# Three of a batch's short float32 runs on the tensor engine are joined to others in a one-core attention and two-MLP kernel

## The chip, the cores and the metric

One core of one Trainium2 chip runs the program. The metric is the device time of one execution in microseconds (us).

## What is computed

Eight batches of attention feed two MLPs in float32. In attention 32 packed queries `p` of each head attend to `k` and `v`; the packed result then serves as keys and values of the attention of `q`:

```python
p_packed = sm_attn(p, k, v)          # 8 batches, 8 heads, 32 rows, 64 wide
out = sm_attn(q, p_packed, p_packed) # 576 rows a head
x = out.transpose(0, 2, 1, 3).reshape(B * S, H * D)   # 4608 x 512
h = x @ w_in                                          # 512 x 2048
g = where(h >= 1, h, where(h <= -1, 0, (h + 1) ** 2 / 4))
x = g @ w_out                                         # 2048 x 512
h = x @ w2_in
y = (h / (1 + exp(-h))) @ w2_out
```

## The kernel before

The MLPs' float32 products are made of three matmul passes over float32r pieces (a high and a low part of each operand). Attention's own matmuls are plain float32.

**Stage A** holds attention and the first MLP. `w_in` is multiplied by `pp` (the packed result) once a batch, so `x @ w_in` needs only the second attention's weights `a2` as its other operand. The stage runs as 256 steps, 32 a batch (16 blocks of 128 columns of `w_in`, for each half `t` of the batch's 576 rows). A step holds one block `h` (`a_h`, 6 matmuls into one PSUM bank) and one block `y` (`a_y`, 12 matmuls that add into four banks of a second pool). Between them work ScalarE (`a_relu`: relu and square; `a_hi`) and VectorE (`a_max`, which is the last to read the bank of `h`; `a_lo`). Block `y` of a step uses what block `h` of four steps earlier made. At the last `y` of a half `t`, `a_y` also copies its four banks out: two copies on VectorE, two on ScalarE.

**Attention of the next batch** is threaded through these steps as a list of slots, one slot a step. `front` has the packed queries: `s1_8` and `s1_end8` (scores), `s1_copy`, `s1_max`, `s1_exp`, transposes `s1_tr` and `s1_trt`, `et_copy` and `ett_copy`, `pp_mm`, `pp_norm`, `pp_tr`, `pp_out`. `back8` has the second attention: scores `s2_8` and `s2_end8`, then transposes and a softmax on VectorE and ScalarE (`t_in` to `t_a2`). `wps` has four pairs of `wp8` (`pp` with 512 columns of `w_in`) and `wp_out` (its split into high and low). All of them, and block `h`, take their PSUM banks with `bank()` from one pool of four (`ps_h`): `s1_8`, `s2_8` and `wp8` take two banks each, `s1_end8`, `s2_end8`, each `s1_tr`, `s1_trt`, `pp_mm` and `pp_tr` one.

**Order.** Each engine takes its instructions in one queue, in an order written out by hand: every piece of work gets a key (its step and a fraction), and all are sorted by key. Within step `n`, `h` and what follows it have fractions from 0.30, attention's slots 0.6 and block `y` with its copies 0.9. So a slot's matmuls stand between an `h` and a `y`. For a batch `b` that begins at step `base + 32`, `G['pf']` is the step, counted from `base`'s batch, of the first slot of `front`, `G['pb']` that of `back8` and `G['pw']` that of the first `wp8`. The same numbers set the steps of the loads (`load_p`, `load_k` four steps ahead of `front`, `load_v` one, `load_win` three ahead of `wp8`). During stage A the weights of the second MLP are also converted and split by ScalarE and VectorE, at steps of their own (`conv_a`, `conv_b`, `a_first` to `a_fourth`).

**Stage B**, the second MLP, follows and is not touched.

Of the kernel before, what the change touches and what calls it, by code (L numbers as in the profile page):

```python
# [72 lines left out]
def attention_then_two_mlps(ctx: ExitStack, tc: tile.TileContext, kT, vv, qT, pT, w_in, w_out, w2_in, w2_out, out):  # L73
# [3 lines left out]
    B, P, NJ, S = kT.shape  # L77
# [13 lines left out]
    NF = DFF // FW  # L91
# [27 lines left out]
    pb = const.tile([P, NJ, N2], F32, name="pbd")  # L119
# [128 lines left out]
    def att_jobs(b):  # L248
# [337 lines left out]
        def J(fn, *a):  # L586
            return lambda: fn(*a)
# [8 lines left out]
            ]),  # L596
            [J(s1_copy, 1), J(s1_max, 0)],
            [J(s1_exp, 0), J(s1_max, 1)],
            [J(s1_exp, 1), J(s1_tr, 0)],
            [J(et_copy, 0), J(s1_tr, 1), J(s1_trt)],  # L600
            [J(et_copy, 1), J(ett_copy), J(s1_rec)],
            [J(pp_mm, 0), J(pp_mm, 1)],
            [J(pp_norm)],
            [J(pp_tr)],
# [1 line left out]
        ]  # L606

        back8 = [
            [J(s2_8)],
            [J(t_in, 0), J(t_in, 1), J(s2_end8)],  # L610
            [J(t_max, 0), J(t_in, 2)],
            [J(t_exp, 0), J(t_max, 1)],
            [J(t_norm, 0), J(t_exp, 1)],
# [157 lines left out]
    def unit_h(i, p, j):  # L771
        return 2 * U * i + 14 * (p // 2) + 2 * j + p % 2

    def unit_o(i, j, p):
        return 2 * U * i + U + NPR * j + p
# [160 lines left out]
                eng.dma_start(out[r:r + P, t, TO[i]:TO[i + 1]], sb.pop(((i, 0, d), name)))  # L936


    G = dict(pf1=4, pb1=18, w1=0, pf=2, pb=16, pw=21, lw=3, lk=4, lv=-1, lq=6, ai=34, ad=25, oraw=1)
    starts = {b: (0,) if b else (0, KF // 2) for b in range(B)}  # L940
    steps = []
    for b in range(B):
# [3 lines left out]
    SPB = 2 * KF  # L946
# [5 lines left out]
    def at(n, fn, *args):  # L952
        ev(n + 0.6, fn, *args)
# [4 lines left out]
    def slots(n, jobs, every=1):  # L958
        for i, slot in enumerate(jobs):
            for fn in slot:  # L960
                at(n + i * every, fn)

    with tc.manual_schedule():
# [3 lines left out]
        for _ in range(10):  # L967
            nc.tensor.matmul(warm[:, :P], ident, ident, start=True, stop=True)
        front, back, wps = att_jobs(0)

        def fill(n, own):
# [36 lines left out]
        def W(f, k, g):  # L1008
            return (f"W{f}.{k}.{g}", wps[f][k][g])
# [63 lines left out]
        for g in range(NG):  # L1073
            for k in range(2):
                n, fn = W(1, k, g)
                job(n, 2 + 0.1 * k + 0.01 * g, fn)
        for f in range(2, NF):
            for g in range(NG):
                for k in range(2):
                    n, fn = W(f, k, g)  # L1080
                    job(n, 4 * f + k + 0.6, fn)
        for i, key in enumerate(ins[2 * KD:]):
            n = i + 3
# [3 lines left out]
        for m in range(4, KF):  # L1087
            n = m - 3 if m < KF // 2 else m + G['oraw'] + 1
            key = ("o", m)
# [10 lines left out]
        def plan_front(b, n):  # L1100
            at(n - G['lk'], load_p, b)
            at(n - G['lk'], load_k, b)
            for g in range(NG):
                at(n + G['lv'] + g, load_v, b, g)
            slots(n, jobs[b][0])

        def plan_back(b, n):
            for g in range(NG + 1):
                at(n - G['lq'] + min(g, 1), load_q8, b, g)
            slots(n, jobs[b][1]())  # L1110

        jobs = {b: att_jobs(b) for b in range(1, B)}
        plan_front(1, G['pf1'])
        plan_back(1, G['pb1'])
# [4 lines left out]
        for b in range(2, B):  # L1119
            base = (b - 1) * SPB  # L1120
            plan_front(b, base + G['pf'])
            plan_back(b, base + G['pb'])
            for f in range(NF):
                n = base + G['pw'] + 4 * f
                for g in range(NG):
                    at(n - G['lw'], load_win, b, f, g)
                slots(n, jobs[b][2][f])
# [34 lines left out]
        for i in range(NBK):  # L1162
            for k in range(2):
                for t in range(2):
                    n = NA - 31.4 + 2 * k + t if i == 0 else K0 + 2 * U * (i - 1) + 4 + 4 * (2 * k + t) + 0.95
# [11 lines left out]
            for p in range(NPR):  # L1177
                b = unit_h(i, p, 0)
# [4 lines left out]
                if p % 2:  # L1183
                    for x, name in enumerate(("t1", "t2", "t3", "t4")):
                        n = unit_o(i, 0, 2) + x if p == NPR - 1 else b + 14 + x // 2
                        bu(n, 20 + x % 2, t_sum, i, p // 2, name)
                for j in range(7):
                    n = unit_o(i, j, p)
# [77 lines left out]
```

## Time and profile before

| what | us |
|---|---|
| time before, median of 3 runs | 1445.77 (1445.53 to 1446.64) |
| the profiled execution's own time | 1445.66 |
| its span | 1443.6 |
| TensorE (PE) busy | 1429.9 |
| VectorE (DVE) busy | 951.3 |
| ScalarE (ACT) busy | 766.2 |

Rows that begin with a time give the start in us from the span's start, how long the merged instructions took, the engine, the line of the kernel, the operation, output and inputs by the program's names, shapes and the count. In brackets stands idle time just ahead of it on that engine, and what ended it. Matmuls are pipelined, so the distance of two starts says what a block cost; the length printed is longer by the last one's tail.

### The profile page before, as it was taken

To read this page: it belongs to the slowest core of one execution; us is meant where nothing else is said; L and a number is where in the kernel's file an instruction comes from. 1 tells how busy PE (TensorE), PEld (TensorE's weight loads), DVE (VectorE), ACT (ScalarE), POOL (GpSimd) and SP (SyncE) were. 2 spreads that over 40 slices of the span, in tenths; PEclk is the share of its full clock that TensorE was granted. 3 is DMA by queue.
4 is the path that set the end of the run, shared out by engine and by line. 5 is a ranking of instruction groups with operands and counts; after the bars stand their busy time and mean duration, and the time that the engine had idled before them with its cause. 6 is when DMAs were issued, how large, how long until landed. Compare 5 with 4: busy or idle time off the path is not lost.

```text
span 1443.6 us, 26352 instructions
## 1 busy us (share of the span) xinstructions
PE 1429.9 (99%) x9812; PEld 1280.5 (89%) x9812; DVE 951.3 (66%) x1711; ACT 766.2 (53%) x1536; POOL 74.8 (5%) x116
## 2 busy tenths in 40 slices
PE   8999999999999999999999999999999999999999
PEld 7778989989899898999998888888888889999998
DVE  5788586675867758577736775477646764774664
ACT  4776667676676767766653452334423541362342
POOL 0250000000000000000000000000000000000000
PEclk9999999999999999999999999999999999999999
DMA  9654545646464555545337677866787678888886
GB/s 346 230 199 131 195 163 185 230 156 222 153 223 162 187 179 190 192 156 185 105 93 241 193 208 222 267 191 193 230 258 195 193 222 281 260 269 285 253 252 223
DMA packets 178639, 300.32 MB, mean 208 GB/s; under 512 B 28624, under 2 KB 76752, under 8 KB 178512
## 3 DMA queue, kind: packets, MB, share of 16 engines
q1 hardware_dynamic: 167760, 264.36, 58.2%
q0 software_dynamic: 9344, 33.04, 6.7%
q8 instruction: 78, 1.28, 0.4%
q10 hardware_dynamic: 1408, 1.25, 0.3%
q14 instruction: 49, 0.40, 0.1%
HBM read 244.97 MB, written 53.61 MB: 207 GB/s over the span
## 4 chain that ended last, share of the span: by engine, by line
PE 90%; DVE 5%; DMA 2%; issue 1%; ACT 1%; POOL 0%; DVEq 0%; ACTq 0%; POOLq 0%
PE ps_y L707 25%; PE ps_o L904 24%; PE ps_h L842 22%; PE ps_h L661 12%; PE ps_wp L573 2%; PE ps_y L703 1%; PE ps_pp L364 1%; DMA qt<-qT 1%; DMA raw<-w_in 1%; DVE g L692 1%; DMA va<-vv 1%; PE ps_s L270 0%; DVE u L682 0%; DVE gt L887 0%; DVE w L154 0%
## 5 line engine op out<-in xcount | busy, mean ns | idle before, releaser
L707 PE MATMUL ps_y<-g,w_o 128*128 128x288 f32 x2976 | 443.8, 298 | 3.0 <-DVE g L692 1.8
L707 PEld LDWEIGHTS ps_y<-g,w_o 128*128 128x128 f32 x2976 | 407.7, 188 | 35.1 <-ACT u L676 10.1
L842 PE MATMUL ps_h<-y,a2r 128*128 128x512 f32 (+1 forms) x1680 | 347.7, 367 | 0.4 <-DVE p L868 0.2
L904 PE MATMUL ps_o<-g,a2r 128*128 128x512 f32 (+1 forms) x1680 | 345.8, 367 | 0.0
L842 PEld LDWEIGHTS ps_h<-y,a2r 128*128 128x128 f32 x1680 | 305.2, 188 | 40.9 <-DVE p L868 1.8
L904 PEld LDWEIGHTS ps_o<-g,a2r 128*128 128x128 f32 x1680 | 305.7, 188 | 39.2
L661 PE MATMUL ps_h<-a,wp 128*128 128x288 f32 x1536 | 246.2, 296 | 1.1 <-DVE u L682 0.4
L682 DVE SCALAR_TENSOR_TENSOR u<-ps_h,u 128x288 f32<-128x288 f32 x256 | 116.1, 455 | 160.2 <-ACT u L677 159.8
L661 PEld LDWEIGHTS ps_h<-a,wp 128*128 128x128 f32 x1536 | 217.3, 188 | 4.4 <-issue 1.6
L676 ACT ACTIVATE u<-ps_h,half 128x288 f32<-128x288 f32 x256 | 128.2, 501 | 171.4 <-PE ps_h L661 147.5
L677 ACT ACTIVATE u<-u 128x288 f32<-128x288 f32 x256 | 113.8, 445 | 8.1
L692 DVE TENSOR_TENSOR g<-u,g 128x288 fp32r<-128x288 f32 x240 | 109.6, 457 | 1.7 <-ACT g L686 1.7
L686 ACT CAST g<-u 128x288 fp32r<-128x288 f32 x248 | 103.5, 417 | 0.2 <-PE ps_y L703 0.2
L800 DVE TENSOR_TENSOR g<-gs,g 128x1024 fp32r<-128x1024 f32 (+1 forms) x80 | 86.7, 1112 | 7.4 <-ACT g L799 7.4
L863 ACT COPY p<-ps_h 128x512 f32<-128x512 f32 (+1 forms) x40 | 21.8, 545 | 124.1 <-PE ps_h L842 116.2
L799 ACT CAST g<-gs 128x1024 fp32r<-128x1024 f32 (+1 forms) x80 | 73.9, 962 | 8.6 <-PE ps_o L904 5.8
L868 DVE TENSOR_TENSOR p<-ps_h,p 128x512 f32<-128x512 f32 (+1 forms) x80 | 50.2, 633 | 39.9 <-PE ps_h L842 39.4
L800 DVE TENSOR_TENSOR g<-gt,g 128x1024 fp32r<-128x1024 f32 (+1 forms) x60 | 64.5, 1112 | 6.8 <-ACT g L799 6.8
L878 ACT ACTIVATE gs<-u 128x512 f32<-128x512 f32 (+1 forms) x40 | 23.6, 589 | 82.6 <-DVE u L868 82.6
L878 ACT ACTIVATE gs<-ps_h 128x512 f32<-128x512 f32 (+1 forms) x40 | 22.3, 556 | 63.3 <-PE ps_h L842 63.3
L799 ACT CAST g<-gt 128x1024 fp32r<-128x1024 f32 (+1 forms) x60 | 53.8, 963 | 0.5 <-PE ps_o L904 0.5
L645 POOL DMA_DIRECT2D win<-win_dram x48 | 25.5, 532 | 515.1 <-DVE g L692 113.2
(142 smaller groups left out, 1145.0 us busy)
## 6 DMA issues: line engine op xcount, KB each, us to landing
a2r<-a_dram SPq DMA_DIRECT2D x280, 256.0 KB, 3.0
a2r<-o_dram SPq DMA_DIRECT2D x280, 256.0 KB, 3.0
win<-win_dram POOLq DMA_DIRECT2D x48, 512.0 KB, 4.3
raw<-w_in SPq DMA_DIRECT2D x32, 512.0 KB, 7.4
raw<-w_out SPq DMA_DIRECT2D x32, 512.0 KB, 6.3
a_dram<-a2w SPq DMA_DIRECT2D x56, 256.0 KB, 2.8
o_dram<-a2w SPq DMA_DIRECT2D x56, 256.0 KB, 2.7
y_dram<-ysb SPq DMA_DIRECT2D x36, 288.0 KB, 2.5
```

Of the source, the lines that this page charges most:

```text
L661: nc.tensor.matmul(ps[:, :HB], w[:, i, o:o + P], a2[:, k, g, :], start=(n == 0), stop=(n == 3 * NG - 1))
L676: nc.scalar.activation(u, h_ps[s][:, :HB], AF.Relu, bias=half, scale=0.5)
L677: nc.scalar.activation(u, u, AF.Square)
L682: nc.vector.scalar_tensor_tensor(u, h_ps.pop(s)[:, :HB], 1.0, u, op0=ALU.max, op1=ALU.min)
L686: nc.scalar.copy(g[:, 0], u_t[s])
L692: eng.tensor_tensor(g[:, 1], u_t.pop(s), g[:, 0].bitcast(F32), op=ALU.subtract)
L707: nc.tensor.matmul(acc["y"][d][:, :HB], w[:, i, d * P:(d + 1) * P], g[:, k], start=(first and n == 0), stop=(last and n == 2),)
L799: nc.scalar.copy(hi, src)
L800: nc.vector.tensor_tensor(lo, src, hi.bitcast(F32), op=ALU.subtract)
L842: nc.tensor.matmul(ps, w[:, x, a * P:(a + 1) * P], b_t[i, j][k][:, a], start=(n == 0 and j in FIRST), stop=(n == 3 * KH - 1), skip_group_c ...
L868: nc.vector.tensor_tensor(t, bk[*key, b][:, :w], x, op=ALU.add)
L904: nc.tensor.matmul(ps, w[:, x, d * P:(d + 1) * P], g[k][:, p % 2], start=(p == 0 and n == 0 and j in FIRST), stop=(p == NPR - 1 and n == 2 ...
```

## The change

For batches 1 to 7 both groups of transposes and `s1_trt` are in one slot, and all three copies of their results in the next. `s2_end8` is in the slot of `s2_8`. For batches 2 to 7 `front` begins three steps earlier (`pf` from 2 to -1), its loads with it. For batches 2 to 6 the last `wp8`, with its load and its `wp_out`, goes from step 33 to step 38 of the batch, the slot of the next batch's `pp_mm`.

```diff
             [J(s1_exp, 0), J(s1_max, 1)],
-            [J(s1_exp, 1), J(s1_tr, 0)],
-            [J(et_copy, 0), J(s1_tr, 1), J(s1_trt)],
-            [J(et_copy, 1), J(ett_copy), J(s1_rec)],
+            *([
+                [J(s1_exp, 1), J(s1_tr, 0)],
+                [J(et_copy, 0), J(s1_tr, 1), J(s1_trt)],
+                [J(et_copy, 1), J(ett_copy), J(s1_rec)],
+            ] if b < 1 else [
+                [J(s1_exp, 1)],
+                [J(s1_tr, 0), J(s1_tr, 1), J(s1_trt)],
+                [J(et_copy, 0), J(et_copy, 1), J(ett_copy), J(s1_rec)],
+            ]),
             [J(pp_mm, 0), J(pp_mm, 1)],
...
         back8 = [
-            [J(s2_8)],
-            [J(t_in, 0), J(t_in, 1), J(s2_end8)],
+            [J(s2_8), J(s2_end8)],
+            [J(t_in, 0), J(t_in, 1)],
             [J(t_max, 0), J(t_in, 2)],
...
-    G = dict(pf1=4, pb1=18, w1=0, pf=2, pb=16, pw=21, lw=3, lk=4, lv=-1, lq=6, ai=34, ad=25, oraw=1)
+    G = dict(pf1=4, pb1=18, w1=0, pf=-1, pb=16, pw=21, lw=3, lk=4, lv=-1, lq=6, ai=34, ad=25, oraw=1)
...
             for f in range(NF):
-                n = base + G['pw'] + 4 * f
+                n = base + (G['pw'] + 4 * f if f + 1 < NF or b + 1 == B else SPB + G['pf'] + 7)
                 for g in range(NG):
                     at(n - G['lw'], load_win, b, f, g)
                 slots(n, jobs[b][2][f])
```

How the instructions stand on TensorE where batch 2 (the first is batch 0) ends its second half (the last `y` of a half reads `w_o_15`). Before, that `y` follows straight on its `h`, and no attention stands there:

```order
L661 MATMUL ps_h_4169<-a2_3841,wp_0_0_3850 128x288 [waits DVE_49]
L661 MATMUL ps_h_4169<-a2_3841,wp_0_0_3850 128x288 x2
L661 MATMUL ps_h_4169<-a2_3841,wp_1_0_3853 128x288 x3
L707 MATMUL ps_y_3617<-g_4088,w_o_15_1291 128x288 [waits Activation_49]
L707 MATMUL ps_y_3617<-g_4088,w_o_15_1291 128x288 x2
L707 MATMUL ps_y_3618<-g_4088,w_o_15_1291 128x288 x3
L707 MATMUL ps_y_3619<-g_4088,w_o_15_1291 128x288 x3
```

In the changed kernel (lines from 602 on have numbers higher by 6) the first scores of batch 4 stand between the two, in `ps_s1_4190`, `ps_s1_4191` and `ps_s1e_4200`; the next `h` is `ps_h_4234`:

```order
L667 MATMUL ps_h_4169<-a2_3841,wp_1_0_3853 128x288 x3
L270 MATMUL ps_s1_4190<-kt_4034,pbd_89 32x512 [waits DMAHW3_49,DMAHW1_49,DVE_49]
L270 MATMUL ps_s1_4191<-kt_4034,pbd_89 32x512 [waits DMAHW2_49,DVE_49]
...
L281 MATMUL ps_s1e_4200<-kte_4036,pbd_89 32x64 [waits DMAHW4_49,DVE_49]
L281 MATMUL ps_s1e_4200<-kte_4036,pbd_89 32x64 x7
L713 MATMUL ps_y_3626<-g_4096,w_o_15_1291 128x288 [waits Activation_49]
L713 MATMUL ps_y_3626<-g_4096,w_o_15_1291 128x288 x2
L713 MATMUL ps_y_3627<-g_4096,w_o_15_1291 128x288 x3
L713 MATMUL ps_y_3628<-g_4096,w_o_15_1291 128x288 x3
L713 MATMUL ps_y_3629<-g_4096,w_o_15_1291 128x288 x3
L667 MATMUL ps_h_4234<-a2_3841,wp_0_1_3993 128x288 [waits DVE_49]
```

The scores moved from behind the third `h` after that `y` to ahead of it; between `ps_h_4169` and `ps_h_4234` three banks of the pool of four are now taken.

On ScalarE at the same place, in the changed kernel, two copies of that last `y` (L722) stand ahead of the relu (L682) of `ps_h_4169`, and the first copies of the scores (L304, L308) behind it:

```order
L722 COPY ysb_4217<-ps_y_3627 128x288
L722 COPY ysb_4227<-ps_y_3629 128x288
L682 ACTIVATE u_4241<-ps_h_4169,half_86 128x288
L683 ACTIVATE u_4241<-u_4241 128x288
L692 CAST g_4244<-u_4176 128x288
L304 COPY s_4187<-ps_s1_4190 128x512
L308 COPY s_4187<-ps_s1e_4200 128x2x64
```

Before, the two copies and this relu stand in the same order; only the score copies are new here.

On VectorE of the changed kernel, at the same place, two copies (L725) stand ahead of the maximum (L688) of `ps_h_4169`, the last reader of its bank:

```order
L725 COPY ysb_4217<-ps_y_3626 128x288
L725 COPY ysb_4227<-ps_y_3628 128x288
L698 TENSOR_TENSOR g_4179<-u_4135,g_4179 128x288
L688 SCALAR_TENSOR_TENSOR u_4241<-ps_h_4169,u_4241 128x288
L698 TENSOR_TENSOR g_4244<-u_4176,g_4244 128x288
```

That order, too, is the one of before; what moved is on TensorE.

## Rows read from the trace of the kernel before

**Rows 1.** The page: busy time by engine, granted clock by slice, the chain by engine.

```profile
PE 1429.9 (99%) x9812; PEld 1280.5 (89%) x9812; DVE 951.3 (66%) x1711; ACT 766.2 (53%) x1536; POOL 74.8 (5%) x116
...
PEclk9999999999999999999999999999999999999999
...
PE 90%; DVE 5%; DMA 2%; issue 1%; ACT 1%; POOL 0%; DVEq 0%; ACTq 0%; POOLq 0%
```

**Rows 2.** Timeline of PE, first attention of batch 4: scores (L270, L281), transposes (L329, L335).

```profile
325.18 0.96 PE L661 MATMUL ps_h<-a,wp 128*128 128x288 f32 x6
326.07 1.09 PE L270 MATMUL ps_s<-kt,pbd 64*32 64x512 f32 x16
327.09 0.43 PE L281 MATMUL ps_s1e<-kte,pbd 128*32 128x64 f32 x16
327.45 1.85 PE L707 MATMUL ps_y<-g,w_o 128*128 128x288 f32 x12
329.14 0.96 PE L661 MATMUL ps_h<-a,wp 128*128 128x288 f32 x6
...
331.54 0.96 PE L661 MATMUL ps_h<-a,wp 128*128 128x288 f32 x6
...
336.32 0.96 PE L661 MATMUL ps_h<-a,wp 128*128 128x288 f32 x6
...
339.18 0.96 PE L661 MATMUL ps_h<-a,wp 128*128 128x288 f32 x6
339.97 0.60 PE L329 MATMUL ps_et<-ident,s 128*128 128x128 f32 x4
340.41 0.38 PE L335 MATMUL ps_ett<-ident,s 128*64 128x128 f32 x2
...
342.21 0.96 PE L661 MATMUL ps_h<-a,wp 128*128 128x288 f32 x6
```

**Rows 3.** Timeline of PE, second scores of batch 4: `s2_8` (L484), `s2_end8` (L495).

```profile
363.46 0.96 PE L661 MATMUL ps_h<-a,wp 128*128 128x288 f32 x6
364.35 1.09 PE L484 MATMUL ps_s<-qt,pp 64*32 64x512 f32 x16
...
367.06 0.96 PE L661 MATMUL ps_h<-a,wp 128*128 128x288 f32 x6
367.95 0.43 PE L495 MATMUL ps_s2e<-qte,pp 128*32 128x64 f32 x16
...
370.00 0.96 PE L661 MATMUL ps_h<-a,wp 128*128 128x288 f32 x6
```

**Rows 4.** Timeline of all engines, last `y` of batch 2's second half and its copies.

```profile
317.60 1.75 PE L707 MATMUL ps_y<-g,w_o 128*128 128x288 f32 x12
...
318.58 0.40 ACT L716 COPY ysb<-ps_y 128x288 f32<-128x288 f32 x1 [1.37 <-PE ps_y L707]
...
319.38 0.40 ACT L716 COPY ysb<-ps_y 128x288 f32<-128x288 f32 x1 [0.40 <-PE ps_y L707]
...
319.68 0.51 ACT L676 ACTIVATE u<-ps_h,half 128x288 f32<-128x288 f32 x1
...
320.69 0.46 DVE L682 SCALAR_TENSOR_TENSOR u<-ps_h,u 128x288 f32<-128x288 f32 x1 [0.89 <-ACT u L677]
```

**Rows 5.** Groups by line: the copies on ScalarE (busy, mean ns, idle before, releaser).

```profile
L716 ACT COPY ysb<-ps_y 128x288 f32<-128x288 f32 x32 | 12.8, 400 | 36.4 <-PE ps_y L707 36.2 <-PE ps_y L703 0.3
```

**Rows 6.** Timeline of DVE beside the second scores of batch 4.

```profile
364.97 0.46 DVE L682 SCALAR_TENSOR_TENSOR u<-ps_h,u 128x288 f32<-128x288 f32 x1 [0.89 <-ACT u L677]
```

**Rows 7.** Timeline of all engines, second scores of batch 1.

```profile
107.67 1.06 PE L661 MATMUL ps_h<-a,wp 128*128 128x288 f32 x6
...
109.20 0.44 DVE L682 SCALAR_TENSOR_TENSOR u<-ps_h,u 128x288 f32<-128x288 f32 x1
...
109.70 0.43 PE L495 MATMUL ps_s2e<-qte,pp 128*32 128x64 f32 x16 [0.97 <-DVE u L682]
```

**Rows 8.** Waits of PE's weight loads, 90 to 720 us: total, times, longest.

```profile
PEld ps_wp L573 <- DVE u L682: 2.2, 4, 1.1
```

## The prediction

> **What bounds the kernel now.** I read the page first: TensorE is busy 1429.9 us of the span and the chain that ended last is 90% PE [rows 1]. What counts is therefore whatever TensorE's queue does between two blocks; work on the other engines costs time only where TensorE waits for it. The granted clock is 9 tenths or more in all 40 slices [rows 1], the higher of its two levels (2.4 GHz), so no term below is a matter of clock.
>
> Then I read TensorE's timeline as distances of starts. An `h` and a `y` with nothing between take 331.54 - 329.14 = 2.40 us [rows 2]. Whatever a pair with an attention run inside takes beyond 2.40 is the price of that run, its way in and out included.
>
> Last I looked for the waits behind TensorE: which reader frees the PSUM bank that the next `h` wants, and what is queued ahead of this reader on VectorE and ScalarE.
>
> **The change part by part.** No matmul is added or removed. Three joints a batch go, and each has a price of its own.
>
> *Second scores in one run.* Split, they cost 367.06 - 363.46 - 2.40 = 1.20 and 370.00 - 367.06 - 2.40 = 0.54 us [rows 3], 1.74 together. The first scores have the same shapes and are already joined: 329.14 - 325.18 - 2.40 = 1.56 [rows 2]. Joining saves 0.18. But `s2_end8` now needs a third bank at once, that of the `h` before last. VectorE's maximum frees it at 364.97 + 0.46 = 365.43 [rows 6], and with the lag of 0.06 from such a release to PE (109.20 + 0.44 to 109.70 [rows 7]) the matmuls start at 365.49. Unhindered they would start 1.02 after `s2_8` (327.09 - 326.07 [rows 2]), at 365.37. That gives back 0.12. Net 0.06 in each of batches 2 to 7: 0.4 us saved, bounds 0 and 6 x 0.18 = 1.1.
>
> *Transposes in one run.* The run of four cost 339.18 - 336.32 - 2.40 = 0.46, that of six 342.21 - 339.18 - 2.40 = 0.63 [rows 2]. Inside a run one transpose takes (340.41 - 339.97) / 4 = 0.11, so ten are worth 1.10 and the two runs cost 1.09. There is no price of a joint here: 0 saved, at most 0.18 a batch if the price of the tiled runs held.
>
> *Last `wp8` beside `pp_mm`.* Both are runs on parts of the array, as the scores are, so I take the same 0.18, five times (batches 2 to 6): 0.9 saved, bounds 0 and 0.9. `wp_out` now comes one step after this run, and the first `h` that reads it a good half step later; between stand `pp_mm`, two `y` and an `h`, at least 2.40 + 1.61 = 4.0 us (below for the 1.61), which hide its two copies and two subtractions. I cost this wait at nothing; splits later than that would cost what they are late, five times. Its load keeps its lead of three steps.
>
> The Trainium skill, "TensorEngine Tiling (Array Packing)", Key Properties, says that changing the tiling mode drains the engine, not the mere step to another tile. By that, `s2_8` to `s2_end8` and `wp8` to `pp_mm` are still changes of mode (64x32 to 128x32 tiles), and a joint would save one border of two, 0.09; the sum would come out 1.0 us higher. The row disagrees in size: the joined first scores hold that same border and are cheaper by the whole 0.18.
>
> *Batch 1.* Its second scores fall where VectorE is behind. Before, an `h` ran at 107.67 and `s2_end8` waited until 109.70 for the maximum that ends at 109.64 [rows 7]. Now the two change places, and this `h` waits for it. It starts 2.03 later, less the 0.54 that `s2_end8` took and the 0.97 of wait that goes [rows 7]: up to 0.5 us worse. Below, -0.2 (only the joint saved). I take +0.4.
>
> *`front` three steps earlier.* This is the part that I find dear. Its first slot moves from step 2 to step -1, that is, to between the last `h` and the last `y` of a half. The first scores take three of four banks and that last `h` holds the fourth. The next `h` must therefore wait until VectorE has taken the maximum of the `h` just ahead of the scores; the order rows show it waiting for VectorE. Where the scores stood before, the maximum had time. Here it is queued behind the copies of the last `y`: ScalarE's relu stands behind two copies, which wait for that `y` (32 such copies idle 36.2 us for PE [rows 5]), and VectorE's maximum waits for relu and square.
>
> The times: `y` starts at 317.60, the second copy on ScalarE at 319.38, the relu at 319.68, the maximum ends at 320.69 + 0.46 = 321.15 [rows 4], 3.55 after the start of `y`. Before, nobody waited for it. Now `y` leaves a tiled run, which makes it 329.14 - 327.45 = 1.69 long instead of 1.61 (a pair's 2.40 less an `h` of 339.97 - 339.18 = 0.79) [rows 2], so the copies come 0.08 later as well and the maximum ends 3.63 after the start of `y`; with the lag of 0.06, `h` starts at 3.69. TensorE is there at 1.69. **Wait: 2.00 us.** Nothing else can run meanwhile, for `h` heads an in-order queue; behind it are the first `y` of the new half and all the rest. ScalarE and VectorE stand idle too, so nothing is caught up.
>
> This holds for the starts of `front` of batches 3 to 7, five places: 10.0 us, between 5 x 1.86 (no lag, no slower `y`) = 9.3 and 5 x 2.2 = 11 (if the first matmul after a gap adds a tenth or two). Batch 2 is spared: there batch 0 ends, whose second half is added up on VectorE (`part_t`), ScalarE copies nothing, and the order gives the next `h` a bank that `s1_copy` frees.
>
> *Loads.* Keys, values and `p` move on SP's queue by the same three steps, past the stores of `ysb` and of the second MLP's weights; their leads stay, four steps (9.6 us) for keys. I cost them at nothing; a late key load would add its lateness once a batch.
>
> **Sum**, against the profiled execution's own 1445.66: +10.0 - 0.4 - 0 - 0.9 + 0.4 = +9.1, 1454.8 us; the median shown lies 0.11 higher, so I say **1454.9**. With the bounds: 9.3 - 1.1 - 1.3 - 0.9 - 0.2 = +5.8, and 11 + 0.5 = +11.5.
>
> **Rivals.**
>
> *The joints are worth what the change counts on, and nothing waits.* Each of 7 + 7 + 5 = 19 joints saves 0.18, 3.4 us: 1442.3, faster by 0.24%. For it: the 0.18 is real for tiled runs. Against: the transposes' rows, and it needs a maximum that ends 2 us sooner than the rows say; it decides if the next `h` in fact gets another bank, or if ScalarE takes the relu ahead of the copies.
>
> *No wait, joints at my prices*: -0.4 - 0.9 + 0.4 = -0.9, 1444.8, no change that can be told.
>
> *The wait and a backlog.* `s1_max`, `wp_out` and `pp_norm` now meet other steps of the weights' conversion on VectorE. Where its queue already runs over, TensorE waits up to 1.1 us at one place [rows 8]. Two such places more: 1457.1.
>
> **How the numbers follow.** What a measurement here can tell from no change is about 0.2%, 2.9 us. My forecast gets 0.74, the backlog 0.10, both slower; the full joints without a wait 0.08, faster; no wait at my prices 0.08, same. So faster 0.08, same 0.08, slower 0.84. The range runs from 1451.5 (the lower bound, +5.8) to 1457.3 (the upper bound and the backlog at two places); the two cases without a wait lie below it.
>
> **What the profile after would show.** Right: five gaps on PE of about 2.0 us ahead of `h`, released by VectorE's maximum (L688), each about 1.7 after the start of a half's last `y`, and hardly elsewhere; the joined second scores 1.6 to 1.7 beyond a plain pair; ten transposes at 1.1; no gap ahead of the `h` that first reads the moved `wp_out`. Wrong: `h` follows that `y` without a gap (then the bank or ScalarE's order is not as I read it), the transposes' joint saves a tenth or more, or the granted clock falls behind the new gaps, which would lengthen everything after them.

## The result, and the profile after

The changed kernel takes **1460.59 us** (median, 1460.1 to 1462.51) against 1446.09 before in the same comparison: a ratio of 1.0103, 95% interval [1.0085, 1.012]. That is 14.5 us slower where 9.1 were forecast, and above the range. The profiled execution is the longest of these, 1462.51 us, 16.85 above that of before.

The page after; its rows answer to [rows 1]:

```profile
PE 1432.1 (98%) x9812; PEld 1282.1 (88%) x9812; DVE 951.3 (65%) x1711; ACT 766.2 (52%) x1536; POOL 75.1 (5%) x116
...
PEclk9999999999999999999999999999999999999999
...
PE 87%; DVE 6%; DMA 3%; ACT 2%; issue 2%; POOL 0%; DVEq 0%; ACTq 0%; POOLq 0%
```

PE is only 2.2 us busier (1429.9 before) in a span that is 17.1 longer: all of the loss but these 2 us is waiting. Who is waited for stands in the view of PE's waits, 90 to 740 us (total, times, longest):

```profile
PE ps_h L667 <- DVE u L688: 11.3, 7, 1.9
...
PE ps_s2e L495 <- DVE u L688: 1.4, 1, 1.4
PE ps_s1e L281 <- DVE u L688: 1.3, 1, 1.3
```

Before, the same view has one short wait of `h` for the maximum (L682 there):

```profile
PE ps_h L661 <- DVE u L682: 0.4, 1, 0.4
```

Five of the seven waits are the predicted places, 1.86 us each; the sixth, 1.59, is at batch 1's second scores, and the last is the short one of before. No `h` waits for the moved `wp_out`, as predicted. Line numbers behind the changed lists are six higher than before: the maximum is L688, the relu L682, the copies of `ysb` L722 and L725. One of the five predicted places in the timeline of all engines, the start of batch 4's `front` (it answers to [rows 2] and [rows 4]):

```profile
323.16 1.09 PE L270 MATMUL ps_s<-kt,pbd 64*32 64x512 f32 x16
...
324.18 0.43 PE L281 MATMUL ps_s1e<-kte,pbd 128*32 128x64 f32 x16
324.54 1.85 PE L713 MATMUL ps_y<-g,w_o 128*128 128x288 f32 x12
...
325.62 0.40 ACT L722 COPY ysb<-ps_y 128x288 f32<-128x288 f32 x1 [2.92 <-PE ps_y L713]
...
326.42 0.40 ACT L722 COPY ysb<-ps_y 128x288 f32<-128x288 f32 x1 [0.40 <-PE ps_y L713]
326.72 0.51 ACT L682 ACTIVATE u<-ps_h,half 128x288 f32<-128x288 f32 x1
...
327.73 0.46 DVE L688 SCALAR_TENSOR_TENSOR u<-ps_h,u 128x288 f32<-128x288 f32 x1 [0.89 <-ACT u L683]
...
328.24 1.06 PE L667 MATMUL ps_h<-a,wp 128*128 128x288 f32 x6 [1.86 <-DVE u L688]
329.14 1.08 PE L713 MATMUL ps_y<-g,w_o 128*128 128x288 f32 x7
```

`y` starts at 324.54; relu follows ScalarE's second copy; the maximum ends at 328.19, 3.65 after the start of `y` (predicted: 3.63); `h` starts 3.70 after it (predicted: 3.69). Where nothing hinders it that is 1.69, so the wait is 2.01. The other four starts of `front` (at 234.84, 417.23, 506.94 and 601.14) show 3.70, 3.71, 3.70 and 3.75. The `h` itself then takes 329.14 - 328.24 = 0.90 in place of 0.80.

The joined runs on PE's timeline: ten transposes, `wp8` with `pp_mm` (both batch 4), second scores (batch 4; they answer to [rows 3]):

```profile
337.91 0.96 PE L667 MATMUL ps_h<-a,wp 128*128 128x288 f32 x6
338.71 1.03 PE L329 MATMUL ps_et<-ident,s 128*128 128x128 f32 x8
339.58 0.38 PE L335 MATMUL ps_ett<-ident,s 128*64 128x128 f32 x2
...
341.39 0.96 PE L667 MATMUL ps_h<-a,wp 128*128 128x288 f32 x6
...
343.79 0.96 PE L667 MATMUL ps_h<-a,wp 128*128 128x288 f32 x6
344.68 1.09 PE L573 MATMUL ps_wp<-win,pp 64*32 64x512 f32 x16
...
349.05 0.96 PE L667 MATMUL ps_h<-a,wp 128*128 128x288 f32 x6
...
370.81 0.96 PE L667 MATMUL ps_h<-a,wp 128*128 128x288 f32 x6
371.70 1.09 PE L484 MATMUL ps_s<-qt,pp 64*32 64x512 f32 x16
372.83 0.43 PE L495 MATMUL ps_s2e<-qte,pp 128*32 128x64 f32 x16
...
374.88 0.29 PE L667 MATMUL ps_h<-a,wp 128*128 128x288 f32 x1
```

Beyond a plain pair of `h` and `y` (2.40): transposes 341.39 - 337.91 - 2.40 = 1.08 (split: 1.09); second scores 374.88 - 370.81 - 2.40 = 1.67 (split: 1.74), where `s2_end8` starts 1.13 behind `s2_8` in place of 1.02; `wp8` with `pp_mm` 349.05 - 343.79 - 2.40 = 2.86, where the trace of before has 1.20 and 1.87 for the two.

So the wait and the joints of batches 2 to 7 are as forecast, and more has gone elsewhere. Starts of `h` after against before, step by step, show where: +1.6 at batch 1's transposes and +0.7 at its second scores; +0.5 some steps behind the second scores of batch 2, where a `y` waits for VectorE; +1.3 at the first scores of batch 5; +1.8 at the second scores of batch 6; +1.5 behind the wait at the start of batch 6's `front`; and +1.1 ahead of step 0, where TensorE, ScalarE and VectorE still run the same instructions as before. The places at batches 5 and 6 are called late places below.

### The profile page after: what moved, and what is told of

It reads as the page before. It is cut to its first block, busy times and chain, and to the rows that moved or that the text cites. A ratio compares the mean times of both kernels' runs of the same rounds, so it can differ in the third digit from the quotient of the medians.

```text
span 1460.7 us, 26346 instructions
## 1 busy us (share of the span) xinstructions
PE 1432.1 (98%) x9812; PEld 1282.1 (88%) x9812; DVE 951.3 (65%) x1711; ACT 766.2 (52%) x1536; POOL 75.1 (5%) x116
## 4 chain that ended last, share of the span: by engine, by line
PE 87%; DVE 6%; DMA 3%; ACT 2%; issue 2%; POOL 0%; DVEq 0%; ACTq 0%; POOLq 0%
PE ps_y L713 24%; PE ps_o L910 24%; PE ps_h L848 22%; PE ps_h L667 12%; PE ps_wp L573 2%; PE ps_y L709 1%; DVE u L688 1%; DMA qt<-qT 1%; PE ps_pp L364 1%; DMA raw<-w_in 1%; DVE g L698 1%; DMA raw<-w_out 1%; ACT u L682 1%; DMA va<-vv 1%; ACT u L683 0%
## 5 line engine op out<-in xcount | busy, mean ns | idle before, releaser
L688 DVE SCALAR_TENSOR_TENSOR u<-ps_h,u 128x288 f32<-128x288 f32 x256 | 116.2, 455 | 170.9 <-ACT u L683 170.3
L682 ACT ACTIVATE u<-ps_h,half 128x288 f32<-128x288 f32 x256 | 128.2, 501 | 175.3 <-PE ps_h L667 149.1
```

Of the source, the lines that this page charges most:

```text
L682: nc.scalar.activation(u, h_ps[s][:, :HB], AF.Relu, bias=half, scale=0.5)
L688: nc.vector.scalar_tensor_tensor(u, h_ps.pop(s)[:, :HB], 1.0, u, op0=ALU.max, op1=ALU.min)
```

## The experiments

The kernel before was measured beside each. Its median was 1445.40 beside joints_only, front_only, batch1_split and relu_first; 1445.47 beside one_step_sooner, raw_early, before_relu_first and best_of_parts; and 1445.53 beside half_the_wait, before_raw_early and best_raw_early. A ratio goes by all executions and not by the two medians.

**joints_only.** `front` and the last `wp8` go back.

```diff
-    G = dict(pf1=4, pb1=18, w1=0, pf=-1, ...)
+    G = dict(pf1=4, pb1=18, w1=0, pf=2, ...)
...
-                n = base + (G['pw'] + 4 * f if f + 1 < NF or b + 1 == B else SPB + G['pf'] + 7)
+                n = base + (G['pw'] + 4 * f if f + 1 < NF or b + 1 == B else G['pw'] + 4 * f)
```

> The two joints alone (transposes in one run, second scores in one run, batches 1 to 7); front and the last wp8 at their old places. By the prediction's terms: second scores -0.4, transposes 0, batch 1's second scores +0.4, together 0: 1446 us. By the trace of after: as that, but batch 1 pays more, its ten transposes take 2.6 us in place of 1.0 because two banks are not free yet, and its second scores net +0.7: 1447 to 1448.5. Rival, each joint worth the 0.18 us of a tiled run: 14 x 0.18 less, 1443.6.

Measured: 1448.04 us (1447.51 to 1449.69), ratio 1.0019 [1.001, 1.0028]. None of the five waits is there, and no joint is worth 0.18. In batches 2 to 7 the starts of `h` move by 0.00 at the transposes (+0.47 from one run, -0.47 from the other) and by -0.07 at the second scores. What is lost is 2.3 us in batch 1 and 0.5 behind batch 2's second scores. This 0.5 is in the trace of every kernel that joins batch 2's scores, and not in front_only. As the traces read, the next `h` comes later behind the joined scores, VectorE stands idle 0.5 us longer there and then has work without a gap until a `y` waits for it; no run tests this reading.

**front_only.** The reverse: `front` and `wp8` moved, the slots of transposes and second scores as before, for all batches.

```diff
-            ] if b < 1 else [
+            ] if b < B else [
                 [J(s1_exp, 1)],
...
-            [J(s2_8), J(s2_end8)],
-            [J(t_in, 0), J(t_in, 1)],
+            [J(s2_8)],
+            [J(t_in, 0), J(t_in, 1), J(s2_end8)],
```

> The earlier front and the moved last wp8 alone; transposes and second scores split as before. By the prediction's terms: five waits +10.0 and -0.9: 1455.2. By the trace of after: five waits with a slower first h, 5 x 2.13 = 10.6, three late places in batches 5 and 6 of 1.3 to 1.8 each, 4.7 together, less 1.0 for wp8: +14.3, 1460.4. If the late places belong to the joined second scores and not to the moved front, one of them (1.8) goes and it is 1458.6.

Measured: 1459.6 us (1458.55 to 1462.7), ratio 1.0103 [1.0088, 1.0119], between the two figures expected. The late place at batch 6's second scores is there too, 1.0 us with split scores in place of 1.8; PE waits 0.6 ahead of batch 5's first scores. So late places come with the moved `front` or the moved `wp8`, and the joined scores make one of them dearer. The ratio is that of the whole change, but the joints still cost something: this trace has two stretches at the lower clock (told of at raw_early), and the trace of after has one behind a wait. Without such stretches, and the one ahead of step 0, the last `h` starts 11.7 us later than before here, 2.5 later in joints_only and 14.8 later in after.

**batch1_split.** After, with `b < 1` turned to `b < 2` in the list of transposes, and the same choice put into `back8`.

```diff
-            ] if b < 1 else [
+            ] if b < 2 else [
                 [J(s1_exp, 1)],
```

> After, with batch 1 alone left as before (its transposes and its second scores split). If the 2 to 3 us that the profile of after has lost by the end of batch 1 come from the joints: 2 to 3 us below after, 1457.6 to 1458.6. If they are a matter of the start's transfers in that one execution: 1460.4 to 1460.8.

Measured: 1458.55 us (1457.6 to 1460.25), ratio 1.0093 [1.0079, 1.0107], 1.5 us below after by the two ratios; in its trace batch 1 costs what it did before, 2.3 us less than in after, but two stretches at a lower clock, told of at raw_early, give some of it back. What the joints did there is seen on PE in the trace of after, batch 1:

```profile
71.27 1.04 PE L329 MATMUL ps_et<-ident,s 128*128 128x128 f32 x8
...
73.86 1.06 PE L667 MATMUL ps_h<-a,wp 128*128 128x288 f32 x6 [1.34 <-DVE wp L137]
...
112.36 1.86 PE L667 MATMUL ps_h<-a,wp 128*128 128x288 f32 x12 [1.59 <-DVE u L688]
```

It is the five waits' mechanism again: ten transposes take three banks at once where they had taken one and two apart, so the next `h` needs a bank that VectorE has not yet read, here that of `wp` (L137). The last row is batch 1's second scores [rows 7], where this was foreseen.

**relu_first.** After, with one order changed: relu, square and maximum of a half's last `h` get keys ahead of the copies of its last `y`.

```diff
+                after_last = h % KF == KF - 1
...
-                    when(h + 1, 1, a_relu, step)
+                    when(*((h, 58) if after_last else (h + 1, 1)), a_relu, step)
...
-                    when(h + 1, 4, a_max, step)
+                    when(*((h, 59) if after_last else (h + 1, 4)), a_max, step)
```

> After, with one order changed: at the end of a half, relu, square and maximum of the last h stand ahead of the copies of the last y on ScalarE and VectorE, not behind them. Front stays three steps earlier and its first scores still take three banks there. Theory, the wait is the queue order of the bank's reader: the five waits of 2.0 us go, and the slow first h with them, 10.6 us less: 1450. Rival, the place itself is dear (three banks taken between two halves, whatever the readers' order): 1458 to 1461. If only relu was late and the maximum still meets the copies, a wait of some 0.5 us stays at each: 1452.5.

Measured: 1446.58 us (1445.84 to 1447.7), ratio 1.0009 [1.0, 1.0018], 3.4 us below what was expected. The same place on the timeline of all engines:

```profile
319.54 0.50 ACT L682 ACTIVATE u<-ps_h,half 128x288 f32<-128x288 f32 x1 [0.58 <-PE ps_h L667]
...
320.55 0.46 DVE L688 SCALAR_TENSOR_TENSOR u<-ps_h,u 128x288 f32<-128x288 f32 x1 [0.86 <-ACT u L683]
320.81 1.89 PE L713 MATMUL ps_y<-g,w_o 128*128 128x288 f32 x12
...
321.92 0.40 ACT L722 COPY ysb<-ps_y 128x288 f32<-128x288 f32 x1 [1.41 <-PE ps_y L713]
...
322.53 0.96 PE L667 MATMUL ps_h<-a,wp 128*128 128x288 f32 x6
```

The maximum ends before the copies begin, and `h` follows 1.72 after the start of `y`, with no wait. The scores stand where they stood, and take as many banks: what was dear is the queue order, not the place. Of the 13.6 us that the ratios differ by, some 10.5 are these five waits with their slow first `h`. The rest was not expected: the late places of after are almost gone from this trace (0.1 and 0.5 us in place of 1.3 and 1.8), and no stretch at the lower clock (below) shows. The joined second scores of batches 3 to 5 and 7 save 0.17 each here, where their third bank, too, comes free sooner.

**one_step_sooner.** After, with `pf` from -1 to -2.

```diff
-    G = dict(pf1=4, pb1=18, w1=0, pf=-1, ...)
+    G = dict(pf1=4, pb1=18, w1=0, pf=-2, ...)
```

> After, with front (and the last wp8 with it) one step sooner still, so that its first scores stand a step ahead of the half's last h and y; the order on ScalarE and VectorE is not touched. Theory, the wait comes from the one maximum that is queued behind the copies of the last y: the next h now wants the bank of an earlier h, whose maximum stands ahead of these copies, so the five waits, the slow first h and the low clock behind them go: 1446.5 to 1449. Rival, any place at a half's end is dear because h meets the copies there anyway: above 1456.

Measured: 1449.62 us (1447.65 to 1451.35), ratio 1.0027 [1.0016, 1.0038], a little above what was expected. Its waits of PE, 90 to 740 us:

```profile
PE ps_h L667 <- DVE u L688: 2.1, 2, 1.6
PE ps_s2e L495 <- DVE u L688: 1.4, 1, 1.4
PE ps_s L270 <- DVE u L688: 0.6, 1, 0.6
```

The five waits go; what `h` still waits for is mostly batch 1's second scores (1.6). Late places (1.4 ahead of second scores, 0.6 ahead of first scores) stay.

**half_the_wait.** After, with relu and square alone moved, the maximum where it was.

```diff
+                after_last = h % KF == KF - 1
...
-                    when(h + 1, 1, a_relu, step)
+                    when(*((h, 58) if after_last else (h + 1, 1)), a_relu, step)
```

> After, with relu and square alone ahead of the copies of a half's last y (ScalarE); the maximum stays behind VectorE's two copies and one subtraction. Theory, the wait is as long as what is queued ahead of the bank's reader: in the trace of after VectorE's subtraction ends 2.3 us after the start of that y, so the maximum ends at 2.75 and h starts at 2.8 in place of 3.7, a wait of 1.1 us at each of the five places: 1446.6 (relu_first) + 5.5 to 6, 1452. Rival, the maximum waits for ScalarE's copies in some other way: 1460. If the low clock behind a wait needs a wait as long as 2 us, no stretch at the lower level; if not, some of the five show one, 1.6 us each in the profile.

Measured: 1454.36 us (1452.71 to 1454.57), ratio 1.0058 [1.0045, 1.007]. On VectorE and PE at the same place:

```profile
322.12 1.89 PE L713 MATMUL ps_y<-g,w_o 128*128 128x288 f32 x12
...
324.02 0.45 DVE L698 TENSOR_TENSOR g<-u,g 128x288 fp32r<-128x288 f32 x1
...
324.38 0.45 DVE L688 SCALAR_TENSOR_TENSOR u<-ps_h,u 128x288 f32<-128x288 f32 x1
...
324.89 0.79 PE L667 MATMUL ps_h<-a,wp 128*128 128x288 f32 x4 [0.89 <-DVE u L688]
```

`h` starts 2.77 after `y`, 1.05 later than in relu_first; so at all five places (1.0 to 1.1). The wait is as long as what is queued ahead of the bank's reader. The time is 2.4 above what was expected: the late places, ahead of the first scores of batch 5 and the second scores of batch 6, cost 1.2 and 1.3 us more in this trace than in relu_first's. No stretch at a lower clock shows.

**raw_early.** After, with the loads of the second MLP's weights one step sooner.

```diff
-                    at(n + 2 * x, load_raw, key)
+                    at(n + 2 * x - 1, load_raw, key)
```

> After, with each load of the second MLP's weights one step (2.4 us) sooner, ahead of the keys on SP's queue; nothing else is changed. Theory, two late places of after (1.2 us ahead of the first scores of batch 5, 1.5 us ahead of the second scores of batch 6) stand behind a ScalarE step that waits for such a load, which the earlier keys delay: both go, the five waits stay: 2.7 us below after, 1457.5 to 1458.2. Rival, they come from the five waits or from the joined scores alone: no change, 1460.5.

What it is about is seen in the trace of after, SP's queue and then ScalarE, VectorE and PE ahead of batch 5's first scores:

```profile
404.25 1.71 SPq L210 DMA_DIRECT2D kt<-kT  x1
406.06 0.53 SPq L170 DMA_DIRECT2D raw<-w_out  x1
...
414.78 0.69 ACT L147 ACTIVATE raw<-raw 128x512 f32<-128x512 f32 x1 [1.80 <-DMA raw<-w_out]
415.37 0.48 ACT L682 ACTIVATE u<-ps_h,half 128x288 f32<-128x288 f32 x1
...
416.35 0.46 DVE L688 SCALAR_TENSOR_TENSOR u<-ps_h,u 128x288 f32<-128x288 f32 x1 [2.03 <-ACT u L683]
...
416.87 0.43 PE L281 MATMUL ps_s1e<-kte,pbd 128*32 128x64 f32 x16 [1.26 <-DVE u L688]
```

A load of weights is issued behind the keys. The first conversion step (L147) heads ScalarE's queue until the load lands, 414.78 - 406.06 = 8.7 us later; the program had given it three steps, 7.2 us. Relu stands behind this step, the maximum behind relu, and PE wants the bank. Before, the keys were three steps later: SP issued this load at 393.09, 12.97 sooner where TensorE was only 7.35 ahead, and it landed in 6.1. So it is now issued 5.6 us later in the course of the steps, and travels 2.6 longer. ScalarE waited 1.6 us in all for such loads between 90 and 740 us, in after 12.6, the most at batch 6's second scores:

```profile
553.97 0.66 ACT L147 ACTIVATE raw<-raw 128x512 f32<-128x512 f32 x1 [4.11 <-DMA raw<-w_out]
```

That load stands behind stores and queries whose steps did not change. It is issued 2.0 us later in the course of the steps than before and takes 9.4 us in place of 7.8; why, was not traced.

Measured: 1458.91 us (1458.41 to 1464.77), ratio 1.0107 [1.0089, 1.0124]. The waits of PE, 90 to 740 us:

```profile
PE ps_h L667 <- DVE u L688: 11.3, 7, 1.9
```

Both late places are gone, as the theory wants, and the five waits stay. But the median is 0.7 above what was expected and two of five executions take 1464.3 and 1464.8, so that the ratio is no better than that of after. The profile is of such a one, and its windows behind the five waits (length, PE busy and matmuls, granted clock, DMA share, GB/s) say why:

```profile
237.10:241.10 4.00, 3.96 (x18) 0.58 0.11 39
328.90:332.90 4.00, 4.00 (x23) 0.62 0.88 330
421.30:425.30 4.00, 4.00 (x19) 0.59 0.09 34
513.30:517.30 4.00, 4.00 (x22) 0.61 0.76 277
605.30:609.30 4.00, 4.00 (x22) 0.63 0.36 123
```

The same of after:

```profile
238.50:242.50 4.00, 3.96 (x29) 1.00 0.11 39
328.20:332.20 4.00, 3.96 (x29) 1.00 0.97 314
420.90:424.90 4.00, 3.96 (x29) 1.00 0.11 39
510.60:514.60 4.00, 3.96 (x18) 0.58 0.92 341
604.90:608.90 4.00, 4.00 (x30) 1.00 0.36 123
```

Behind all five waits of this execution, and behind one of five in after, the granted clock is at the lower level (1.2 GHz) for most of the window, and 18 to 23 matmuls are done where 29 or 30 are at the higher (2.4 GHz). From the first `h` behind the wait to the second after it 6.42 us pass in place of 4.88: 1.5 us for each fall, 7.7 for five.

**before_relu_first** and **before_raw_early.** The kernel before with relu_first's diff, and with raw_early's.

> The kernel before, with relu, square and maximum of a half's last h ahead of the copies of its last y, as in relu_first. Theory: before, no h waits for that maximum, so nothing is gained: a ratio of 0.9995 to 1.0005. Rival, this order is worth something of its own (ScalarE and VectorE less behind after each half), in which case relu_first's gain is not a measure of the five waits: 0.997 or less.

> The kernel before, with each load of the second MLP's weights one step sooner. Theory, its ScalarE waits only 1.6 us for such loads and PE's waits behind VectorE there are no matter of loads: 0.9993 to 1.0003. Rival, the sooner loads are worth 1 us or more by themselves: below 0.999.

Measured: 1445.28 us, ratio 0.9999 [0.999, 1.0008], and 1445.45 us, 0.9999 [0.999, 1.0008]. Neither edit is worth anything by itself that can be told (to about 0.1%); their gains in after are what the moved `front` and `wp8` had cost.

**best_of_parts** and **best_raw_early.** After with the diffs of relu_first and batch1_split; the second with raw_early's as well.

> relu_first and batch1_split together: the moved front and wp8, joints in batches 2 to 7 only, and relu, square and maximum of a half's last h ahead of the copies of its last y. By the terms measured: relu_first's 1.2 us over before, less 2.25 that batch 1's joints cost: 1 us under before, a ratio of 0.9993. Rival, batch 1's joints lose nothing outside a profile: as relu_first, 1.0008.

> best_of_parts and raw_early together. Theory, the 1.3 and 1.0 us that best_of_parts still waits ahead of first and second scores stand behind late loads of the second MLP's weights and go: 1445.0 - 2.3, a ratio of 0.998 to 0.9985. Rival, these waits come in other places then or the earlier loads cost as much elsewhere: 0.9995 to 1.0005.

Measured: 1445.0 us (1443.77 to 1447.17), ratio 0.9998 [0.999, 1.0007], and 1444.02 us (1443.33 to 1445.21), 0.9989 [0.998, 0.9998]. The first lies between theory and rival, with the theory's 0.9993 inside its interval; it still waits 1.3 us ahead of batch 5's first scores. With the sooner loads this wait is gone. The 1.0 ahead of second scores stays: it is batch 1's, as before [rows 7], and no matter of loads. So 0.9989 lies between the two ranges expected. It is 1.5 us under before, and the interval ends just below 1. The starts of `h` in this trace agree: five joints of `wp8` at 0.2 and second scores at 0.17 each, 2.1 together, less the 0.5 behind batch 2. The joints are thus worth about a thousandth, at the limit of what these runs can tell, once nothing else pays for them.

## Why the prediction was too low

The mechanism of the five waits, their places and their size were right; the sum was 5.4 us short, since other terms were put at nothing or not seen. Term by term, for the profiled execution, from the starts of `h`:

| term | predicted | measured |
|---|---|---|
| five waits | +10.0 | +10.1 (5 x 2.02) |
| slower first `h` behind them | in the upper bound alone | +0.5 (5 x 0.10) |
| second scores, batches 2 to 7 | -0.4 | -0.4 (6 x 0.07) |
| transposes, batches 2 to 7 | 0 | 0 |
| `wp8` beside `pp_mm` | -0.9 | -1.0 (5 x 0.21) |
| batch 1's second scores | +0.4 | +0.7 |
| batch 1's transposes | 0 | +1.6 |
| a `y` behind batch 2's second scores | not seen | +0.5 |
| loads | 0 | +3.1 (1.3 and 1.8) |
| low clock behind a wait | 0 | +1.5 (one fall) |

These come to 16.6; 1.1 more lie ahead of step 0, where the clock of this one execution is at the lower level between 33 and 37 us. joints_only and best_raw_early show this stretch too and the others don't; the instructions there are the ones of before, so I don't count it to the change. Together 17.7, where the last `h` of stage A starts 17.4 later than before and the time is 16.85 longer: the terms are read to some tenths each. In the median, 1.9 lower, this stretch and the fall behind the wait have less weight; none of the other three executions was profiled, so its 14.5 can't be split.

**The step that failed is "Loads. I cost them at nothing."** It asked whether the loads that move keep their leads; they do. It did not ask which loads that don't move now come late: those of the second MLP's weights, which share SP's queue. That they are the cause of both late places is shown, for sooner loads alone take both away. The term was put at 0 and measured 3.1, about what the median lies above the range (3.3). How they come late is seen for batch 5 alone, behind the keys. There the moved last `wp8` adds a second suspect: its two `win` loads now go out at 399.20 and 400.72, beside the first of these weights and the keys. No run moves one without the other. The rival with the backlog had two late places, at 1.1 us each; that there are two is luck. It put them down to VectorE's own steps, where the cause is ScalarE's wait for a DMA, and it took the 1.1 from a row of PE's weight loads [rows 8], while the matmuls themselves waited 0.2 us in all there. The range took this backlog and the upper bound each by itself; their sum, 1459.5, would have fallen short too.

**"Transposes in one run: 0 saved"** held for batches 2 to 7. For batch 1 the price of banks, worked out for the scores, was not asked of the transposes: three banks at once, and an `h` that waits 1.34 us for `wp`'s reader. At its second scores `h` does start 2.03 later, as worked out, but less is won back: 0.7 lost, above the bound of 0.5.

**The wait** was sized to 0.05 us at each place, and all of its reading is borne out: relu_first takes it away by order alone, half_the_wait halves it, one_step_sooner moves the scores from under it. The fall of the clock behind it, named in the prediction as what would make it wrong, came in some executions, so that a place cost 2.1 us with its slow first `h`, or 3.6 with a fall.

**The joints.** Second scores joined are worth 0.18 less the 0.11 that the third bank costs, as worked out; in relu_first, where the bank comes sooner, they are worth 0.17. The Trainium skill, "TensorEngine Tiling (Array Packing)", Key Properties, says that a change of the tiling mode drains the engine; the prediction worked out from it that a joint of two modes saves half, 0.09. No run here bears the half out: `wp8` with `pp_mm` saved 3.07 - 2.86 = 0.21, and the unhindered scores 0.18. The 0.18 was itself measured on a run that changes from 64x32 to 128x32 tiles inside, so the rows gave no ground for halving it.

What stays open: why the clock falls behind one wait and not behind another of the same length, five of five in one execution and one of five in another; why SP comes late to the load ahead of batch 6's second scores; and why such loads, for which ScalarE waits 10.8 us in all in relu_first, hardly hold up PE there. No run set any of these apart.

## What to carry to other kernels

Where blocks are joined so that more banks are taken at once, look up who frees the next bank and what stands ahead of this reader in its own queue; that wait, here 2 us, was ten times what a joint saves (0.2), and moving the reader up cost nothing that could be measured. When work moves earlier, its loads move past other loads in the same queue: check when those are issued and needed, too. A wait of TensorE may cost more than its length: in ten of twenty places here the clock fell behind it, 1.5 us each. And equal times need not be lost in the same way: front_only and the whole change have one ratio, but different waits and different falls of the clock.

## What the runs showed of the hardware that was not expected

Behind gaps of 1.86 us on TensorE, all at the starts of `front`, the granted clock fell to the lower level (1.2 GHz) at some places and not at others: 5 of 5 (raw_early), 1 of 5 (after), 2 of 5 each (front_only, batch1_split). Behind the 0.89 us gaps of half_the_wait, at the same places, it fell at none of 5, and behind the gaps of 1.26 to 1.59 elsewhere in after at none. Each fall cost 1.5 us. The page can't show it: its row of the clock prints 9 in all 40 slices in each of these profiles, and only narrow windows tell.

Loads of 512 KB of the second MLP's weights took 3.6 to 9.7 us from issue to landing in the trace of before and 3.7 to 10.3 in that of after (90 to 740 us); 10 of 32 took over 7.2 in both. A lead of 7.2 us was thus exceeded before, too, almost without a wait of ScalarE (1.6 us).
